# Attention row sums: fewer tile pairs summed by DMA, partition folds set further apart, the last folds done on 32 rows in DRAM

## The chip, the cores and the metric

The kernel runs on one core of one Trainium2 chip. The metric is the device time of one execution in microseconds; three runs of the kernel before give a median of 1814.33 us (1810.88 to 1819.57). TensorE (PE in the profile) multiplies, ScalarE (ACT) computes exponentials and copies out of PSUM, VectorE (DVE) adds, GpSimd (POOL) and SyncE (SP) issue DMAs. Each engine works through its own queue in the order of the program and waits on semaphores of the others.

## The reference

A gated mixture: attention over 32 heads of width 32 and a layer of small experts, mixed by a gate per token. What the change touches is the softmax's denominator in `_A_ref`, the sum of `exp(scores)` over the 2048 keys, for each head and query:

```python
x = A_x                                                  # 1 x 2048 x 1024
g = _sigmoid((x * gate_w).sum(-1, keepdims=True))
# _A_ref
qkv = (x @ wqkv).reshape(B, S, 3, H, Dh).transpose(2, 0, 3, 1, 4)    # H = 32, Dh = 32
scores = jnp.einsum("bhqd,bhkd->bhqk", q, k) * (Dh ** -0.5)
p = _softmax(scores, axis=-1)
a = jnp.einsum("bhqk,bhkd->bhqd", p, v).transpose(0, 2, 1, 3).reshape(B, S, D) @ wo
# _B_ref: two top-1 choices of 8 for each of 32 router heads, one of 64 experts, gelu(x . u_e) * v_e
return g * a + (1 - g) * b
```

## The kernel before

The kernel computes the projections first (to about 630 us of the span), then attention head by head (to about 1624 us), then the output product with `wo`. All of the program's order is written out by hand; the tile framework adds the semaphores.

**Attention.** For a head `h` the keys are in 16 tiles of 128 (`NT` = 16), the queries in 4 quarters of 512 (`NQ` = 4). One tile of one head is one *step*; step `k = h * 16 + kt`, 512 steps in all. `scores` (L1289 and L1298) multiplies a key tile by the queries, a quarter at a time, into a ring of seven PSUM banks, and ScalarE writes the exponentials as a tile `P[h, kt]` of 128 keys x 2048 queries (1 MB). `pv` (L1310) multiplies the tile by the values. Scores and `pv` are issued alternately in batches of about nine quarters; after each batch the actions due at the steps that it finished are issued (`at(step, f, ...)` puts them there, the list `todo` holds them), and then `presum` for the step itself. So the step of an action sets its place in every queue, and each queue keeps that order.

**Row sums.** The sum of `P[h, :]` over all keys is made in three levels.

1. *Over the 16 tiles.* VectorE adds tile after tile into `ACC[h]` (`presum` and `add`, L1351: two instructions of 128 x 1024 for each tile). Some pairs of tiles are first added by DMA: `accumulate(h, b, a)` (L1340) has GpSimd's queue add `P[h, a]` to `P[h, b]` in place, four steps after `b`'s number as listed (at `base + b + 4`), and VectorE adds the sum later (`add_pair`, and `merge` for the last pair). `pairs_of` names the pairs: (0, 2), (4, 6), (8, 10) in a head with three, (0, 2), (8, 10) in a head with two. Before, the odd heads below 28 have two, the others three; head 31 has its own. The tiles that are in no pair are added at their own step. `merge_odd` of head 29 is two adds of 64 partitions, each as long as one of 128.
2. *Over the 128 partitions of `ACC[h]`.* `fold(h, n)` (L1368) is a DMA on GpSimd's queue that adds partitions n to 2n - 1 to partitions 0 to n - 1; each fold waits for the one before it. Before: n = 64, 32, 16, then `store_rows` (L1372) writes 16 partitions to DRAM, `SED[g]`. Four heads make a group `g`.
3. *In DRAM.* `fold_rows(g, n)` (L1375) adds rows n to 2n - 1 of the group to rows 0 to n - 1, a DMA from DRAM to DRAM: n = 8, 4, 2, 1. `load_r` reads the row that is left, and `norm_r` (L1406 and L1407) makes reciprocals, times the gate, and stores them (`RD`), to be multiplied into the attention output at the end.

Heads 28 to 31 go another way: `head_sums` and `rowsum` (L1323) sum over the partitions on TensorE, partly after `fold_odd` (L1363) put two heads in one tile.

**Places.** The tiles `P` live in 13 places, 11 from head 20 step 8 on, and 10 from head 27 step 11 on. `p_tile` gives a new tile the place whose planned end is nearest, `min(until)`; the planned end of a tile is its step plus 14 for the tile `b` of a pair, 10 for a tile `a`, 5 for any other. The plan is only a choice of place: the exponential that writes a tile waits until every reader of the place's earlier tile is done (VectorE's add, `pv`, the DMA that reads it).

**Queues.** GpSimd's queue issues the pair sums, folds, stores and row folds, in order; an issue that waits holds those behind it. SyncE's queue loads queries, keys and values of later heads, stores the heads' outputs and, before, issued `load_r`.

Of the kernel before, what the change touches and what calls it, by code (L numbers as in the profile page):

```python
# [17 lines left out]
S = 2048  # L18
# [14 lines left out]
def gated_mha_peer_kernel(ctx, tc, xT, wqkv, wv, wo, wq, k12, ug, v, out):  # L33
# [23 lines left out]
    SMD = [dram.tile([4, S], F32, name=f"smd{g}") for g in range(G)]  # L57
    SED = [dram.tile([16, 4, S], F32, name=f"sed{g}") for g in range(G - 1)]
    RD = dram.tile([G, 4, S], F32, name="rd")
# [1091 lines left out]
    def pairs_of(h):  # L1151
        if h == H - 1:
            return (2, 4), (2, 6)
        if h % 2 and h < H - 4:
            return (0, 2), (8, 10)
        return (0, 2), (4, 6), (8, 10)
# [213 lines left out]
    def store_rows(h):  # L1370
        g, j = divmod(h, 4)
        nc.gpsimd.dma_start(SED[g][:, j, :], ACC.pop(h)[:16])  # L1372

# [26 lines left out]
    def load_r(g):  # L1400
        R[g] = wk.tile([128, 128], F32, name="rr", bufs=1)[:, :64]
        dma(R[g], (SMD[g] if g == G - 1 else SED[g][0]).rearrange("j (b m) -> (j b) m", m=64))

    def norm_r(g):
        r = R.pop(g)
        nc.vector.reciprocal(r, r)  # L1406
        nc.vector.tensor_mul(r, r, G64)  # L1407
        dma(RD[g].rearrange("j (b m) -> (j b) m", m=64), r)
# [43 lines left out]
    def at(step, f, *a):  # L1452
        todo.setdefault(step, []).append((f, a))

    for h in range(H):
# [6 lines left out]
        if h < H - 1:  # L1462
            at(base + 12, add_pair, h, 0)
            if len(pairs_of(h)) == 3:
                at(base + NT + 1, add_pair, h, 1)
            at(base + NT, finish, h)
            at(base + NT + 5, merge_odd if h == H - 3 else merge, h)
            if h == H - 2:
                at(base + NT + 8, head_sums, h)
            elif h == H - 3:  # L1470
                at(base + NT + 7, fold_odd, h)
                at(base + NT + 14, head_sums, h - 1, 2)
# [344 lines left out]
```

## Time and profile before

| | us |
|---|---|
| median of three runs | 1814.33 |
| lowest, highest run | 1810.88, 1819.57 |
| profiled execution | 1813.28 |
| its span | 1811.1 |
| TensorE, ScalarE, VectorE, GpSimd busy in it | 1798.6, 1218.4, 1485.4, 299.6 |
| DMA bytes moved | 361.66 MB |

The span runs from the first to the last instruction of the profiled execution; its time is 2.2 us longer. Busy time is counted over the whole span, although the stages differ: during attention TensorE, ScalarE and VectorE are all above 90%. A line of a timeline has start, length, engine, line, operation, what it writes and reads, how many instructions were merged into it, and in brackets the engine's idle time before it with what ended it. A line of a table of waits has who waited for whom, the sum in us, how often, and the longest. A line of DMA issues has destination and source, queue, how many, KB each, and the median from issue to landing.

### The profile page before, as it was taken

What the parts mean: (1) busy time and instruction counts of PE and PEld (TensorE: products, weight loads), DVE (VectorE), ACT (ScalarE), POOL (GpSimd) and SP (SyncE); (2) the same over time, 40 slices, a digit from 0 to 9 for tenths busy, and PEclk for the clock granted to TensorE, in tenths of its full rate; (3) what the DMA queues carried; (4) which work ended last, traced back from release to release, by engine and by line L of the source; (5) the groups of instructions that cost most, each with busy time, mean ns of one, the idle gap of its engine ahead of it and who ended that gap; (6) DMA issues with size and microseconds to landing.
All of it is one profiled execution on the core that took longest, in us unless ns stands there. A gap on an engine that the chain in (4) does not pass through costs nothing.

```text
span 1811.1 us, 27980 instructions
## 1 busy us (share of the span) xinstructions
PE 1798.6 (99%) x10567; PEld 1137.5 (63%) x10567; DVE 1485.4 (82%) x1656; ACT 1218.4 (67%) x1608; POOL 299.6 (17%) x370
## 2 busy tenths in 40 slices
PE   9999999999999999999999999999999999999999
PEld 7777777788888755555555555455544555447887
DVE  7868685368987689998989989898999898994584
ACT  4434422211233499999999999999999999992221
POOL 0222000026401211112112121121121211210000
PEclk9999999999999999999999999999999999999999
DMA  7788888723248689999999989999999899967871
GB/s 244 232 284 265 278 247 300 257 71 106 82 140 272 231 193 187 182 177 200 200 196 193 207 184 212 191 178 207 201 195 214 193 190 211 199 151 206 268 181 58
DMA packets 132753, 361.66 MB, mean 200 GB/s; under 512 B 18388, under 2 KB 58724, under 8 KB 107128
## 3 DMA queue, kind: packets, MB, share of 16 engines
q0 software_dynamic: 22752, 133.22, 38.7%
q1 hardware_dynamic: 89704, 190.71, 35.8%
q10 hardware_dynamic: 20160, 35.92, 6.8%
q8 instruction: 84, 1.38, 0.3%
q14 instruction: 53, 0.43, 0.1%
HBM read 172.58 MB, written 78.98 MB: 139 GB/s over the span
## 4 chain that ended last, share of the span: by engine, by line
PE 94%; DMA 3%; issue 1%; DVE 1%; ACT 1%; ACTq 0%; SPq 0%; DVEq 0%; POOL 0%; POOLq 0%
PE ring L1289 27%; PE o L1310 24%; PE bk L155 13%; PE bk L711 10%; PE pa L155 6%; PE bk L758 5%; PE bk L926 2%; PE pa L1561 2%; PE bk L311 2%; PE bk L491 1%; DMA P<-P 1%; PE bk L395 1%; DMA wo_raw<-P 1%; PE pa L1568 1%; DMA smd<-ssb 1%
## 5 line engine op out<-in xcount | busy, mean ns | idle before, releaser
L1298 ACT ACTIVATE P<-ring 128x512 f32<-128x512 f32 (+3 forms) x999 | 816.0, 938 | 17.8 <-PE ring L1289 9.6
L1351 DVE TENSOR_TENSOR acc<-acc,P 128x1024 f32<-128x1024 f32 x414 | 477.1, 1219 | 28.5 <-DMA P<-P 14.2
L1310 PE MATMUL o<-P,V 128*32 128x512 f32 (+1 forms) x4024 | 417.3, 534 | 0.0
L1289 PE MATMUL ring<-Q,K 98*128 98x512 f32 x1024 | 270.5, 407 | 1.7 <-ACT P L1298 1.7
L1289 PE MATMUL ring<-z,z 98*128 98x512 f32 x1020 | 267.4, 406 | 0.1
L1289 PEld LDWEIGHTS ring<-Q,K 98*128 98x128 f32 x1024 | 182.8, 188 | 120.9 <-ACT P L1298 42.1
L1289 PEld LDWEIGHTS ring<-z,z 98*128 98x128 f32 x1020 | 182.1, 188 | 114.7 <-ACT P L1298 40.0
L1310 PEld LDWEIGHTS o<-P,V 128*32 128x32 f32 x4024 | 111.7, 109 | 220.2 <-issue 200.4
L1351 DVE TENSOR_TENSOR rb<-rb,P 128x1024 f32<-128x1024 f32 x186 | 214.4, 1219 | 5.8 <-ACT P L1298 4.1
L240 ACT ACTIVATE hi<-bk 128x512 fp32r<-128x512 f32 x40 | 23.7, 594 | 120.4 <-PE bk L711 102.2
L1298 ACT ACTIVATE wo_raw<-ring 128x512 f32<-128x512 f32 (+3 forms) x110 | 100.4, 986 | 1.6 <-PE ring L1289 1.0
L711 PE MATMUL bk<-xh,e 128*128 128x512 f32 x384 | 94.2, 394 | 0.0
L1368 POOL DMA_DIRECT2D acc<-acc x58 | 48.3, 832 | 275.2 <-DMA acc<-acc 120.8
L711 PE MATMUL bk<-xl,e 128*128 128x512 f32 x384 | 92.2, 389 | 0.0
L711 PEld LDWEIGHTS bk<-xh,e 128*128 128x128 f32 x384 | 71.0, 188 | 22.0 <-issue 3.4
L253 DVE TENSOR_TENSOR lo<-bk,hi 128x512 fp32r<-128x512 f32 x40 | 27.6, 690 | 69.4 <-ACT hi L240 68.0
L1351 DVE TENSOR_TENSOR acc<-acc,wo_raw 128x1024 f32<-128x1024 f32 x56 | 65.9, 1219 | 21.4 <-DMA wo_raw<-P 16.8
L1340 POOL DMA_DIRECT2D P<-P x60 | 64.3, 1072 | 106.2 <-PE o L1310 51.0
L711 PEld LDWEIGHTS bk<-xl,e 128*128 128x128 f32 x384 | 72.1, 188 | 15.0
L101 DVE TENSOR_TENSOR e<-wraw,e 128x512 fp32r<-128x512 f32 (+3 forms) x64 | 54.9, 865 | 25.2 <-ACT e L100 24.7
L1298 ACT ACTIVATE vhl<-ring 128x512 f32<-128x512 f32 (+3 forms) x83 | 71.0, 939 | 0.2
L155 PE MATMUL bk<-xh,e 128*128 128x512 f32 x288 | 68.5, 393 | 0.0
(305 smaller groups left out, 2442.9 us busy)
## 6 DMA issues: line engine op xcount, KB each, us to landing
P<-P POOLq DMA_DIRECT2D x60, 1024.0 KB, 14.7
wqt<-in_wq SPq DMA_DIRECT2D x26, 1024.0 KB
wraw<-in_wqkv SPq DMA_DIRECT2D x30, 512.0 KB
acc<-acc POOLq DMA_DIRECT2D x20, 512.0 KB, 11.4
wo_raw<-P POOLq DMA_DIRECT2D x10, 1024.0 KB, 14.9
qdh<-hi ACTq DMA_DIRECT2D x32, 256.0 KB
qdl<-lo ACTq DMA_DIRECT2D x32, 256.0 KB
kdh<-hi ACTq DMA_DIRECT2D x32, 256.0 KB
```

What stands on the lines that cost most here:

```text
L101: (on or nc.vector).tensor_tensor(out=lo, in0=src, in1=hi.bitcast(F32), op=OP.subtract)
L155: nc.tensor.matmul(ps, self.a[a][i][:, k, :], self.b[b][j][k], start=(not first and k == 0 and i == j == 0), stop=(k == HC - 1 and i == 1))
L311: nc.tensor.matmul(ps[32 * quad:32 * quad + 32, :], kpad[:, quad % 2, i, :], t[:, quad, :], start=(i == 0), stop=(i == 3))
L711: nc.tensor.matmul(ps, t[:, kc // HC, a, kc % HC], x_at(b, n, kc), start=first, stop=last)
L758: nc.tensor.matmul(ps, x_at(a, t // 4, kc)[:, tok], b, start=first, stop=last)
L926: nc.tensor.matmul(p, x_at(a, t // 4, kc)[:, tok], b, start=first, stop=last)
L1289: on_ring(nc.tensor.matmul(ring[:, i, :], K[:98, kt * 128:(kt + 1) * 128], Q[:98, qc * 512:(qc + 1) * 512], start=True, stop=True), i)
L1298: on_ring(nc.scalar.activation(P[h, kt][:, q0 * 512:(q0 + m) * 512].rearrange("p (a m) -> p a m", a=m), ring[:, i:i + m, :], AF.Exp, scale ...
L1310: nc.tensor.matmul(O[h][32 * qc:32 * qc + 32, c0:c1], Vt[g][:, kt, 32 * j:32 * j + 32], p[:, qc * 512 + c0:qc * 512 + c1], start=(kt == 0) ...
L1340: nc.gpsimd.dma_start(P[h, b], P[h, a], accum_op=OP.add)
L1351: nc.vector.tensor_add(out[:, c], a[:, c], b[:, c])
L1368: nc.gpsimd.dma_start(ACC[h][:n], ACC[h][n:2 * n], accum_op=OP.add)
```

## The change

- `pairs_of`: two pairs instead of three in heads 2, 6, 10, 14, 18, 22, 26 and 30. Only every fourth head and head 29 keep three; the tiles 4 and 6 of those eight heads are added by VectorE one by one.
- The sum of the first pair is taken at step 14 (three pairs) or 16 (two) instead of 12, the second at 18 instead of 17, the merge at 22 instead of 21, and the planned end of a tile `b` is 16 steps on instead of 14.
- Fold 64 stands at step 24 instead of 23, fold 32 at 32 instead of 28, the fold to 16 rows is gone, and the store, now of 32 rows, is at 40 instead of 37.
- In DRAM the folds are of 16, 8, 4 and 2 rows, eight steps apart instead of five (five in the last such group), and two rows are left. `load_r` reads both side by side, by GpSimd's queue in the last group, and `norm_r` adds them on VectorE.
- One load of reciprocals for the end (`load_rb`) stands at step 13 of head 31 instead of 8.

```diff
-    SED = [dram.tile([16, 4, S], F32, name=f"sed{g}") for g in range(G - 1)]
+    SED = [dram.tile([32, 4, S], F32, name=f"sed{g}") for g in range(G - 1)]
...
-        if h % 2 and h < H - 4:
+        if h % 4 and h != H - 3:
             return (0, 2), (8, 10)
         return (0, 2), (4, 6), (8, 10)
...
-        until[i] = k + (14 if kt in [b for b, _ in pairs] else 10 if kt in [a for _, a in pairs] else 5)
+        until[i] = k + (16 if kt in [b for b, _ in pairs] else 10 if kt in [a for _, a in pairs] else 5)
...
-        nc.gpsimd.dma_start(SED[g][:, j, :], ACC.pop(h)[:16])
+        nc.gpsimd.dma_start(SED[g][:, j, :], ACC.pop(h)[:32])
...
     def load_r(g):
-        R[g] = wk.tile([128, 128], F32, name="rr", bufs=1)[:, :64]
-        dma(R[g], (SMD[g] if g == G - 1 else SED[g][0]).rearrange("j (b m) -> (j b) m", m=64))
+        R[g] = wk.tile([128, 128], F32, name="rr", bufs=1)
+        if g == G - 1:
+            dma(R[g][:, :64], SMD[g].rearrange("j (b m) -> (j b) m", m=64))
+        else:
+            dma(R[g].rearrange("p (r m) -> p r m", r=2), SED[g][:2].rearrange("r j (b m) -> (j b) r m", m=64),
+                nc.gpsimd if g == G - 2 else nc.sync)
 
     def norm_r(g):
-        r = R.pop(g)
+        r = R[g][:, :64]
+        if g < G - 1:
+            nc.vector.tensor_add(r, r, R[g][:, 64:])
+        R.pop(g)
         nc.vector.reciprocal(r, r)
...
-            at(base + 12, add_pair, h, 0)
-            if len(pairs_of(h)) == 3:
-                at(base + NT + 1, add_pair, h, 1)
+            three = len(pairs_of(h)) == 3
+            at(base + (14 if three else 16), add_pair, h, 0)
+            if three:
+                at(base + NT + 2, add_pair, h, 1)
             at(base + NT, finish, h)
-            at(base + NT + 5, merge_odd if h == H - 3 else merge, h)
+            at(base + NT + 6, merge_odd if h == H - 3 else merge, h)
...
-                at(base + NT + 7, fold, h, 64)
+                at(base + NT + 8, fold, h, 64)
                 if g + 1 < G:
-                    at(base + NT + 12, fold, h, 32)
-                    at(base + NT + 17, fold, h, 16)
-                    at(base + NT + 21, store_rows, h)
+                    at(base + 2 * NT, fold, h, 32)
+                    at(base + 2 * NT + 8, store_rows, h)
         if j == 3 and g + 1 < G:
-            for i, n in enumerate((8, 4, 2, 1)):
-                at(base + NT + 26 + 5 * i, fold_rows, g, n)
-            at(base + NT + 46, load_r, g)
-            at(base + NT + 53, norm_r, g)
+            gap = 5 if g == G - 2 else 8
+            for i, n in enumerate((16, 8, 4, 2)):
+                at(base + 2 * NT + 14 + gap * i, fold_rows, g, n)
+            at(base + 2 * NT + 14 + 4 * gap, load_r, g)
+            at(base + 2 * NT + 14 + 5 * gap + (2 if gap == 5 else 0), norm_r, g)
...
-    at((H - 1) * NT + 8, load_rb, 0, KC - 2, KC - 1)
+    at((H - 1) * NT + 13, load_rb, 0, KC - 2, KC - 1)
```

More of the change, by code (lines that the diff above doesn't have):

```diff
@@ L1462, in gated_mha_peer_kernel @@
         if h < H - 1:
-            at(base + 12, add_pair, h, 0)
-            if len(pairs_of(h)) == 3:
-                at(base + NT + 1, add_pair, h, 1)
+            three = len(pairs_of(h)) == 3
+            at(base + (14 if three else 16), add_pair, h, 0)
+            if three:
+                at(base + NT + 2, add_pair, h, 1)
             at(base + NT, finish, h)
-            at(base + NT + 5, merge_odd if h == H - 3 else merge, h)
+            at(base + NT + 6, merge_odd if h == H - 3 else merge, h)
             if h == H - 2:
-                at(base + NT + 8, head_sums, h)
+                at(base + NT + 9, head_sums, h)
             elif h == H - 3:
-                at(base + NT + 7, fold_odd, h)
-                at(base + NT + 14, head_sums, h - 1, 2)
+                at(base + NT + 8, fold_odd, h)
+                at(base + NT + 15, head_sums, h - 1, 2)
             else:
-                at(base + NT + 7, fold, h, 64)
+                at(base + NT + 8, fold, h, 64)
                 if g + 1 < G:
-                    at(base + NT + 12, fold, h, 32)
-                    at(base + NT + 17, fold, h, 16)
-                    at(base + NT + 21, store_rows, h)
+                    at(base + 2 * NT, fold, h, 32)
+                    at(base + 2 * NT + 8, store_rows, h)
         if j == 3 and g + 1 < G:
-            for i, n in enumerate((8, 4, 2, 1)):
-                at(base + NT + 26 + 5 * i, fold_rows, g, n)
-            at(base + NT + 46, load_r, g)
-            at(base + NT + 53, norm_r, g)
+            gap = 5 if g == G - 2 else 8
[3 more added lines that the diff above has]
+            at(base + 2 * NT + 14 + 5 * gap + (2 if gap == 5 else 0), norm_r, g)
         if g + 1 < G:
```

## The prediction

> **What bounds the kernel now.** I read the page first, then the attention stage (about 633 to 1624 us) by windows of one head, then the chain of waits, then the timelines around each place where the chain leaves TensorE.
>
> ```profile
> PE 1798.6 (99%) x10567; PEld 1137.5 (63%) x10567; DVE 1485.4 (82%) x1656; ACT 1218.4 (67%) x1608; POOL 299.6 (17%) x370
> ```
> ```profile
> 1407.40:1438.30 30.90, 30.90 (x220) 15.67 (x216) 29.07 (x26) 30.46 (x42) 6.22 (x8) 1.00 0.86 185
> 1531.20:1562.20 31.00, 29.90 (x199) 13.90 (x195) 23.31 (x22) 27.27 (x33) 4.88 (x6) 0.94 1.02 193
> sum 990.60, PE 988.91 PEld 496.31 DVE 913.36 ACT 971.27 POOL 178.04; mean PE 30.90 PEld 15.51 DVE 28.54 ACT 30.35 POOL 5.56
> ```
>
> The columns after the times are PE, PEld, DVE, ACT and POOL busy, granted clock, DMA share, GB/s. Over 32 heads TensorE is idle 1.7 us of 990.6. Nothing in the change takes a matmul away, so attention can be shortened only where TensorE was held up. The chain has one block of ten score matmuls per head, which serves as a clock:
>
> ```profile
> 850.20 2.59 PE ring L1289 x10
> 881.14 2.60 PE ring L1289 x10
> ...
> 1221.76 2.60 PE ring L1289 x10
> ...
> 1315.15 2.59 PE ring L1289 x10
> ...
> 1439.06 2.59 PE ring L1289 x10
> 1470.83 2.60 PE ring L1289 x10
> 1501.78 2.59 PE ring L1289 x10
> 1521.78 19.73 DMA P<-P
> ...
> 1567.40 2.60 PE ring L1289 x10
> ```
>
> Twelve heads from 850.20 to 1221.76 take 30.96 us each, 1.935 us a step (16 steps to a head). 1221.76 to 1315.15 is 0.5 over three such heads, 1439.06 to 1470.83 0.8 over one, 1501.78 to 1567.40 3.7 over two. **Held up: 5.0 us in all**, and 3.7 of it is one event:
>
> ```profile
> 1519.80 0.78 POOL L1368 DMA_DIRECT2D acc<-acc  x1 [10.89 <-PE o L1310]
> 1521.78 0.90 POOL L1340 DMA_DIRECT2D P<-P  x1 [1.20 <-ACT P L1298]
> 1529.58 0.78 POOL L1368 DMA_DIRECT2D acc<-acc  x1 [6.90 <-DVE acc L1351]
> ```
> ```profile
> 1541.59 1.88 ACT L1298 ACTIVATE P<-ring 128x2048 f32<-128x2048 f32 x1 [1.43 <-DMA P<-P]
> ```
> ```profile
> 1541.70 0.73 PE L1289 MATMUL ring<-Q,K 98*128 98x512 f32 x2
> 1543.52 2.95 PE L1289 MATMUL ring<-Q,K 98*128 98x512 f32 x7 [1.10 <-ACT P L1298]
> 1546.41 3.17 PE L1310 MATMUL o<-P,V 128*32 128x512 f32 x16
> ```
> ```profile
> 1532.16 2.36 DVE L1351 TENSOR_TENSOR rb<-P,P 128x1024 f32<-128x1024 f32 x2 [0.61 <-ACT P L1298]
> 1541.60 2.36 DVE L1351 TENSOR_TENSOR acc<-acc,P 128x1024 f32<-128x1024 f32 x2 [7.08 <-DMA P<-P]
> ```
>
> The mark at 1501.78 stands at step 4.5 of head 28, so its tile 10 is written 6.5 steps on, at 1514.4. The pair DMA of tiles 8 and 10 goes out at 1521.78, right behind the 32-row fold of head 27 (which waits for fold 64 to land; its row names a matmul that ended just then), and lands at 1541.5. ScalarE needs the place of one of its tiles and waits 1.43; TensorE then idles 1.10 and runs its next matmuls slowly (the window's clock is 0.94). So 1.43 us of waiting cost 3.7: 2.3 on top. The 0.5 is a place that VectorE gave back late, without a slow clock, at 1285 us: 0.4 us of ScalarE's waiting cost 0.5.
>
> ```profile
> ACT P L1298 <- DVE rb L1351: 0.4, 1, 0.4
> ```
>
> **The change part by part.** *POOL queue.* The 16-row fold is gone for 28 heads, and fold 64, fold 32 and the store now stand eight steps (15.5 us) apart. Before, each stood five steps (9.7 us) behind a DMA that it waits for, with the pair DMAs queued behind it:
>
> ```profile
> POOL acc L1368 <- DMA acc<-acc: 120.8, 19, 10.6
> POOL sed L1372 <- DMA acc<-acc: 83.5, 14, 10.5
> POOL rb L1368 <- DMA rb<-rb: 65.6, 11, 9.6
> ```
> ```profile
> P<-P POOLq DMA_DIRECT2D x60, 1024.0 KB, 14.7
> acc<-acc POOLq DMA_DIRECT2D x20, 512.0 KB, 11.4
> acc<-acc POOLq DMA_DIRECT2D x19, 256.0 KB, 7.8
> acc<-acc POOLq DMA_DIRECT2D x19, 128.0 KB, 9.9
> sed<-acc POOLq DMA_DIRECT2D x19, 128.0 KB, 9.0
> sed<-sed POOLq DMA_DIRECT2D x7, 256.0 KB, 8.9
> sed<-sed POOLq DMA_DIRECT2D x7, 128.0 KB, 13.0
> ```
>
> With 15.5 us between them a fold of 11.4 and one of 7.8 are down before the next asks, so pair DMAs go out when due: in head 28 at about 1514.4, not 7 us later. Pair sums get 10 to 12 steps (19.4 to 23 us) from issue to use instead of 8 or 9 (15.5 to 17.4), against 14.7 to land. The wait of 7.08 and the 3.7 go, and most likely the 0.5 and the 0.8 with them: **-5.0 us**. Bounds: -5.0, since no more was lost, and 0, if the same waits come back elsewhere. Eight pair DMAs of 1 MB and 28 folds of 128 KB go; 28 stores double to 256 KB, and the row folds of a group grow from 480 to 960 KB: 8.0 + 3.5 - 3.5 - 3.3, so the queue's bytes fall by nearly 5 MB, which the bound of 5.0 already holds.
>
> *VectorE.* Each head that loses a pair adds one tile more, eight heads in all. The pace, twenty halves without a break:
>
> ```profile
> 1543.88 22.79 DVE L1351 TENSOR_TENSOR rb<-rb,P 128x1024 f32<-128x1024 f32 x20
> ```
>
> That is 2.28 us a tile. A head with three pairs needs 12 adds (27.4 us), with two 13 (29.6) of 30.96, so VectorE still fits; the eight added sums cost 0 while the matmuls cover them (18.2 us if they did not). The extra 128x64 sum in norm_r is nearest to the multiply beside it, seven times 0.22 us, off the path:
>
> ```profile
> 1602.23 0.22 DVE L1407 TENSOR_TENSOR rr<-rr,G 128x64 f32<-128x64 f32 x1
> ```
>
> *Places.* This is where I see the cost. A tile's place is taken by a later tile, and ScalarE may write there only when the last reader is done. I laid out the rule of p_tile with the new 16/10/5. In a two-pair head the first pair sum is now VectorE's last item at step 16. VectorE works from the end of the exp of step 3 (1.9 us after it begins, as in the 128x2048 row above) through 13 adds: done 1.9 + 29.6 = 31.5 us after step 3 began, and its place goes to step 3 of the next head, 30.96 after, in heads 27 and 28 (ten or eleven places; earlier heads have at least a step more). About 0.7 us of waiting with the hand-over, twice. At the price of the small holds (0.4 cost 0.5) **+1.6 us**; bounds 0 (the ring's seven banks absorb it) and +6 (each draws the 2.3 of slow clock).
>
> Head 30 is worse. Between step 3 of head 30 and its own first pair sum VectorE has 14 adds: eleven single steps, two for merge_odd of head 29, and the sum itself: done at 1.9 + 31.9 = 33.8. The place goes to step 2 of head 31, 15 steps on: 29.0, plus the row sums put in before it:
>
> ```profile
> 1589.06 1.04 PE L1323 MATMUL ring<-acc,ones 128*32 128x512 f32 x8
> ```
>
> 30.1, so ScalarE waits about 3.8 us. Before, that head had 9 adds for singles, and the last of its pairs was due a step later into step 4. With the slow clock of the 1541 event, 3.8 + 2.3 = **+6.1 us**; bounds +2 (the ring hides most, no slow clock) and +9.
>
> *Fold behind the merge.* The merge moves from step 5, ahead of that step's add, to step 6, behind it: fold 64 and the next pair DMA wait in POOL's order until about 11 us after step 3 in a three-pair head; before, the pair went out about 8 after. Landing 14 to 18 later (14.7 median; eight pairs fewer speak for the short end), tile 6 of head 29 is free at 25 to 29; step 0 of head 30 wants it 13 steps on, at 25.2. Bounds 0 and +4 + 2.3; I take **+1.0**.
>
> *DRAM rows.* Sixteen rows of 32 KB are folded, then 8, 4 and 2. The first is bounded by 8.9 (256 KB) and twice that; with steps of 8 (15.5 us) nothing queues behind it, and with 5 in the last group it can hold POOL by up to 8 us, which the pair of head 30 can take. 0 here, a rival below.
>
> *End.* VectorE's last sum and the row sums that need it:
>
> ```profile
> 1617.80 9.16 DVE L1351 TENSOR_TENSOR acc<-acc,P 128x1024 f32<-128x1024 f32 x8
> ```
> ```profile
> 1627.47 1.92 PE L1323 MATMUL o<-P,ones 128*32 128x512 f32 x16
> 1629.21 1.04 PE L1323 MATMUL o<-acc,ones 128*32 128x512 f32 x8
> ...
> 1652.79 2.07 PE L1561 MATMUL pa<-woh,z 128*128 128x512 f32 x4 [4.16 <-ACT z L100]
> ```
>
> The sum is done at 1627.0, TensorE asks at 1629.2: 2.2 us spare, about one add, and the wait in head 31 gives VectorE time to catch up. Bounds 0 and +1; 0.
>
> Sum: -5.0 + 1.6 + 6.1 + 1.0 = **+3.7 us**. The profiled execution took 1813.28 (span 1811.1 and 2.2 around it), which gives 1817.0; the median of the runs, 1814.33, lies 1.05 above it, so I forecast **1818.0**.
>
> The Trainium skill ("TensorE: Matmul & The Clock Gate", Part 1) has the matmul clock fall to half only after an idle window of about 3.4 us, and rise again after as long. The trace disagrees: 1.10 us of idle was followed by slow matmuls. By that rule the wait of 3.8 alone would be slow, for one window at half rate, an estimate of 1.7 us in place of 2.3, and the sum +3.1.
>
> **The rivals.** (1) *The new waits do not bind*: TensorE runs seven banks ahead and ScalarE's wait is swallowed, while the old 5.0 goes. For it: 1.7 us idle in 990. Against it: 1.43 of ScalarE's waiting cost 3.7. -5.0 + 1.5 gives 1811. (2) *Places run out late*, the one on the slower side: from head 25 with ten or eleven places the pair DMAs of tiles 4 and 6, sent 3 us later, land 18 after; steps 1 of head 29 and 0 of head 30 wait 2 and 4 us, each with 2.3 of slow clock, 10.6 in place of 1.0: +13.3, 1828. It decides once such a pair lands more than 14 us after issue; the median of 14.7 speaks for it, the emptier queue against. (3) *The row folds are late*: the last group's chain of four, 13.0 each, plus its load exceed the 27 steps (52 us) up to norm_r, which stands before VectorE's adds of head 31; 4 x 13.0 and 7.8 for the load (as the 256 KB fold) are 60, 8 us late, 1826. Against it: the 256 KB row fold landed in 8.9, and 4 x 8.9 + 7.8 fits. (4) *Nothing happens*: the old waits return in the same size, 1814.
>
> **How the numbers follow.** Forecast 0.48, (1) 0.20, (2) 0.22, (3) 0.05, (4) 0.05. About 0.5% (9 us) is what this measurement can tell from no change. The forecast's own range is 1813 to 1823; reaching to (1) and most of (2) gives 1809 to 1829. Faster needs 1805.3, more than all that was held up: 0.04, for gains I do not see. Slower, above 1823.4: most of (2) and (3), the upper end of the forecast: 0.29. The rest is 0.67.
>
> **What would show it.** Right: the marks 30.96 apart up to head 26; POOL's waits for acc<-acc and rb<-rb near nothing; no wait of VectorE for P<-P; waits of ScalarE's P on VectorE's acc or rb of some 0.7 us near 1467 and 1498 and of about 4 near 1595, the last with a clock below 1. Wrong: no such wait near 1595, or a wait on DMA P<-P near 1557, or marks that spread before head 20.

## The result, and the profile after

| | before | after |
|---|---|---|
| median of 22 runs each, side by side | 1814.53 us | 1816.63 us |
| lowest, highest run | 1810.21, 1822.80 | 1812.08, 1819.19 |
| ratio after to before, 95% interval | | 1.0007 (0.9997 to 1.0017) |
| profiled execution, its span | 1813.28, 1811.1 us | 1816.48, 1814.7 us |
| VectorE, GpSimd busy in it | 1485.4, 299.6 us | 1503.8, 270.8 us |

No difference that this measurement can tell; the forecast was 1818.0. (The ratio is estimated from all runs; it is not the quotient of the two medians, 1.0012, which lies inside its interval.) The small result is made of two larger terms, and the profile shows both. First the marks of the chain of waits, one block of ten score matmuls per head, in the changed kernel:

```profile
1222.74 2.59 PE ring L1289 x10
...
1315.65 2.59 PE ring L1289 x10
...
1439.62 2.59 PE ring L1289 x10
1470.58 3.07 PE ring L1289 x10
1502.04 3.22 PE ring L1289 x10
1533.65 2.60 PE ring L1289 x10
1564.65 2.59 PE ring L1289 x10
```

1222.74 to 1315.65 is 30.97 a head, and so it goes on to 1470.58: the 0.5 at head 21 and the 0.8 at head 26 are gone. So is the 3.7 behind head 28 (1533.65 to 1564.65 is 31.0). New are 0.5 and 0.65 (31.46 and 31.61 for one head, with longer blocks at their start). GpSimd's waits and its DMAs' landings (tables of waits and of DMA issues, attention stage) say why the old ones went:

```profile
POOL acc L1368 <- DMA acc<-acc: 8.5, 7, 2.1
POOL rb L1368 <- DMA rb<-rb: 2.6, 2, 2.2
```
```profile
P<-P POOLq DMA_DIRECT2D x59, 1024.0 KB, 9.6
acc<-acc POOLq DMA_DIRECT2D x20, 512.0 KB, 5.4
```

120.8 us of waiting for acc<-acc are 8.5 now, 65.6 for rb<-rb are 2.6, and the same 1 MB pair DMA lands in 9.6 us instead of 14.7. VectorE has no wait for a DMA left in attention. ScalarE waits for a place three times, and each time for VectorE; its timeline:

```profile
1468.84 1.88 ACT L1298 ACTIVATE P<-ring 128x2048 f32<-128x2048 f32 x1 [0.60 <-DVE rb L1351]
...
1500.45 1.88 ACT L1298 ACTIVATE P<-ring 128x2048 f32<-128x2048 f32 x1 [0.76 <-DVE acc L1351]
...
1596.23 0.60 ACT L1298 ACTIVATE P<-ring 128x512 f32<-128x512 f32 x1 [4.50 <-DVE acc L1351]
```

Step 3 of heads 27 and 28, step 2 of head 31, as laid out. (TensorE's row sums of heads 28 to 30, `head_sums` with `fold_odd`, also stand one step later, which the list of the change leaves out.) VectorE's timeline shows that it never rests ahead of the third: nine adds on end, the pair sum of head 30 as the last of them.

```profile
1575.61 20.53 DVE L1351 TENSOR_TENSOR acc<-acc,P 128x1024 f32<-128x1024 f32 x18
1596.05 2.36 DVE L1351 TENSOR_TENSOR acc<-P,P 128x1024 f32<-128x1024 f32 x2
```

TensorE's timeline there; of ScalarE's 4.50 us of waiting 3.39 and 0.23 reach it:

```profile
1596.88 0.74 PE L1289 MATMUL ring<-Q,K 98*128 98x512 f32 x1 [3.39 <-ACT P L1298]
1597.85 0.79 PE L1289 MATMUL ring<-Q,K 98*128 98x512 f32 x1 [0.23 <-ACT P L1298]
1598.58 3.64 PE L1310 MATMUL o<-P,V 128*32 128x512 f32 x16
1602.15 2.86 PE L1289 MATMUL ring<-Q,K 98*128 98x512 f32 x8
1604.94 1.92 PE L1310 MATMUL o<-P,V 128*32 128x512 f32 x16
```

The same sixteen matmuls take 3.64 us and, six microseconds on, 1.92. **Attention as a whole**, from the first exponential of its stage to the copy of the last head's output, is a length that every experiment below is read by. In the changed kernel:

```profile
628.07 2.15 ACT L1298 ACTIVATE P<-ring 128x512 f32<-128x512 f32 x2 [1.62 <-PE ring L1289]
...
1629.08 0.60 ACT L1387 ACTIVATE osb<-o 128x512 f32<-128x512 f32 x1 [1.66 <-PE o L1310]
```

1001.0 us; before, 1624.66 - 627.29 = 997.4 by the same two rows. That is +3.6, where the sum of the prediction was +3.7; how its terms make it up is in the part on the prediction. From that copy to the end of the span, *the rest*, there are 185.6 us, before 186.5.

### The profile page after: what moved, and what is told of

It reads as the page before. It is cut to its first block, busy times and chain, and to the rows that moved or that the text cites. A ratio compares the mean times of both kernels' runs of the same rounds, so it can differ in the third digit from the quotient of the medians.

```text
span 1814.7 us, 27897 instructions
## 1 busy us (share of the span) xinstructions
PE 1799.9 (99%) x10567; PEld 1138.0 (63%) x10567; DVE 1503.8 (83%) x1679; ACT 1217.9 (67%) x1608; POOL 270.8 (15%) x335
## 4 chain that ended last, share of the span: by engine, by line
PE 96%; DMA 2%; ACT 1%; issue 1%; DVE 0%; SPq 0%; ACTq 0%; DVEq 0%
PE ring L1289 28%; PE o L1310 25%; PE bk L155 13%; PE bk L711 10%; PE pa L155 6%; PE bk L758 5%; PE bk L926 2%; PE bk L311 2%; PE pa L1569 2%; PE bk L491 1%; PE bk L395 1%; PE pa L1576 1%; ACT P L1298 1%; DMA wraw<-in_wqkv 1%; DMA smd<-ssb 1%
## 5 line engine op out<-in xcount | busy, mean ns | idle before, releaser
L1298 ACT ACTIVATE P<-ring 128x512 f32<-128x512 f32 (+3 forms) x990 | 807.9, 939 | 20.9 <-PE ring L1289 9.6
L1351 DVE TENSOR_TENSOR acc<-acc,P 128x1024 f32<-128x1024 f32 x420 | 484.1, 1220 | 22.1 <-ACT P L1298 22.0
L1351 DVE TENSOR_TENSOR rb<-rb,P 128x1024 f32<-128x1024 f32 (+1 forms) x188 | 217.2, 1220 | 8.4 <-ACT P L1298 8.4
L1340 POOL DMA_DIRECT2D P<-P x59 | 53.6, 909 | 469.5 <-PE o L1310 171.2
L1298 ACT ACTIVATE wo_raw<-ring 128x512 f32<-128x512 f32 (+3 forms) x119 | 105.7, 971 | 1.1 <-PE ring L1289 0.2
L1298 ACT ACTIVATE vhl<-ring 128x512 f32<-128x512 f32 (+3 forms) x83 | 72.8, 951 | 1.4 <-PE ring L1289 0.9
L100 ACT ACTIVATE e<-wraw 128x512 fp32r<-128x512 f32 (+3 forms) x64 | 44.7, 705 | 38.7 <-DMA wraw<-in_wqkv 22.5
```

What stands on the lines that cost most here:

```text
L100: nc.scalar.activation(hi, src, AF.Copy)
L1298: on_ring(nc.scalar.activation(P[h, kt][:, q0 * 512:(q0 + m) * 512].rearrange("p (a m) -> p a m", a=m), ring[:, i:i + m, :], AF.Exp, scale ...
L1340: nc.gpsimd.dma_start(P[h, b], P[h, a], accum_op=OP.add)
L1351: nc.vector.tensor_add(out[:, c], a[:, c], b[:, c])
```

## The experiments

Theory: the added time is ScalarE waiting for places whose last reader is a late pair sum, and the 5.0 us gained are GpSimd's queue, whose issues the change sets further apart (*the spread* below). Main rival: VectorE with 13 adds to a head is too full, whatever their order. Each run was timed beside the kernel before, which had medians of 1815.47 (sum14, sum14_h30, end20, spread_only), 1814.27 (pure_spread, pairs_only, late_h30, sum14_copy) and 1812.95 us (end21, spread_sum12, fold27, before_copy). Each group ran on another chip. So medians of different groups can differ by some 2.5 us for no reason in the kernel, and are better compared by how far each lies below the kernel before beside it. The table has what the profiles gave: attention and the rest as above, then the issue of one DMA near the end, the 1 MB copy `t3l<-t2l`, against the end of attention, and the time from the issue of the last row sums' store `smd<-ssb` (8 KB) to that of the load behind it, which waits for it to land. Both become important below. (Where the first expectations count "the stretch behind attention" at 178.5 us, they count to the last block of matmuls; the rest, to the end of the span, is about 7 us longer.)

| run | median us | ratio to before (95%) | attention | rest | copy issued | store to load |
|---|---|---|---|---|---|---|
| before | 1814.53 | | 997.4 | 186.5 | +4.8 | 10.4 |
| after | 1816.63 | 1.0007 (0.9997 to 1.0017) | 1001.0 | 185.6 | +4.9 | 10.5 |
| sum14 | 1808.95 | 0.9954 (0.9938 to 0.9970) | 992.6 | 185.4 | +4.9 | 10.5 |
| sum14_h30 | 1810.98 | 0.9973 (0.9957 to 0.9989) | 993.6 | 187.4 | +4.9 | 11.3 |
| late_h30 | 1819.04 | 1.0018 (1.0001 to 1.0036) | 1002.1 | 187.8 | +4.9 | 11.8 |
| end20 | 1809.35 | 0.9957 (0.9938 to 0.9977) | 992.7 | 186.0 | +4.0 | 12.4 |
| end21 | 1802.16 | 0.9941 (0.9920 to 0.9963) | 992.5 | 179.6 | -2.0 | 7.1 |
| pure_spread | 1810.19 | 0.9973 (0.9961 to 0.9985) | 993.5 | 186.6 | +4.8 | 10.7 |
| spread_only | 1805.33 | 0.9936 (0.9910 to 0.9961) | 995.6 | 179.9 | -3.5 | 7.1 |
| spread_sum12 | 1802.19 | 0.9941 (0.9919 to 0.9962) | 992.6 | 179.5 | -4.0 | 7.3 |
| pairs_only | 1809.20 | 0.9968 (0.9946 to 0.9989) | 998.1 | 182.8 | -0.1 | 8.8 |
| fold27 | 1814.02 | 1.0012 (0.9991 to 1.0033) | 992.9 | 188.4 | +4.9 | 12.3 |
| sum14_copy | 1806.36 | 0.9950 (0.9930 to 0.9970) | 992.8 | 184.9 | +26.6 | 9.2 |
| before_copy | 1813.20 | 1.0004 (0.9987 to 1.0021) | 1000.7 | 181.7 | +24.8 | 7.5 |

### The late pair sums

**sum14**, the changed kernel with

```diff
-            at(base + (14 if three else 16), add_pair, h, 0)
+            at(base + 14, add_pair, h, 0)
```

> The changed kernel with one number altered: in every head the first pair sum stands at step 14 in VectorE's order, as it already does in heads of three pairs, and not at step 16. Theory (the added time is the wait of ScalarE for places whose last reader is VectorE's last item): the pair sum is done two adds, 4.6 us, earlier; the waits of 0.6 and 0.76 us in heads 27 and 28 go, the wait of 4.5 in step 2 of head 31 falls below 0.7, the clock in that window comes back above 0.97, and the time is some 8 us below the changed kernel, near 1808.5, so 0.9965 of the kernel before, with the 5.0 us of the POOL queue's spread left as the gain. Rival (VectorE with 13 adds a head is simply too full, whatever their order): the same sums are only handed on, waits of the same size turn up at the places of later tiles, and the time stays within 2 us of 1816.6.

As the theory had it. VectorE does the same adds, in another order, and all three waits are gone: in ScalarE's table of waits the writing of `P` at L1298 has one line left, and it names TensorE.

```profile
ACT P L1298 <- PE ring L1289: 7.5, 31, 1.6
```

7.7 us of the median follow (1816.63 to 1808.95; 8.6 when each is set against the kernel before beside it), 8.4 of attention. VectorE's load is not what binds; the rival falls.

**sum14_h30**, the same in head 30 alone (`14 if three or h == H - 2 else 16`):

> The same edit in head 30 alone. Theory: the two small waits of heads 27 and 28 stay (0.6 and 0.76 us, some 1.2 us of time) and only the 7.1 us at head 31 go, so about 7 us below the changed kernel, near 1809.6. Rival (the small waits weigh more than their length, as places that are late are handed on from head to head): 1811 to 1813. Rival (VectorE too full): 1816.6.

Attention is 993.6: 7.4 us less than in the changed kernel for head 31 alone. The waits of 0.6 and 0.8 us at heads 27 and 28 stay, and cost 993.6 - 992.6 = 1.0. The time, 1810.98, is 1.4 above the 1809.6 expected; it would fit the first rival's 1811 as well. Attention decides: it is where the theory has it, and the profiled execution is longer in the rest, whose store took 11.3 us here.

**late_h30**, head 30's first pair sum one tile later still:

```diff
-            at(base + (14 if three else 16), add_pair, h, 0)
+            at(base + (14 if three else 18 if h == H - 2 else 16), add_pair, h, 0)
```

> The changed kernel with the first pair sum of head 30 one tile add later still in VectorE's order (behind the first sum of head 31). Theory (ScalarE's wait in step 2 of head 31 is this sum's lateness, and time follows it one for one): the wait grows from 4.5 to 6.8 us, and the time by 2.3 us, to 1818.9; the slow clock behind it stays at about 2.5 us. Rival (the wait is set by something else, VectorE's load in all or a DMA): wait and time as in the changed kernel. Rival (a longer idle stretch of TensorE costs more in slow clock): over 4 us more.

The wait is the sum's lateness, to the tenth: 6.75 us, one add of 2.28 more than 4.50.

```profile
1598.51 0.60 ACT L1298 ACTIVATE P<-ring 128x512 f32<-128x512 f32 x1 [6.75 <-DVE acc L1351]
```

The time came out as expected (1819.04, +2.4), but not for the reason given. Between the two profiled executions, which are 3.3 apart, attention grew by 1.1 us only; the other 2.2 are in the rest, with a store of 11.8 us, and what part of those is chance stays open. Why attention grew by half of the wait is in TensorE's timeline and in its granted clock, microsecond by microsecond. This run:

```profile
1599.16 0.80 PE L1289 MATMUL ring<-Q,K 98*128 98x512 f32 x1 [5.67 <-ACT P L1298]
1600.14 0.79 PE L1289 MATMUL ring<-Q,K 98*128 98x512 f32 x1 [0.18 <-ACT P L1298]
1600.87 3.26 PE L1310 MATMUL o<-P,V 128*32 128x512 f32 x16
```
```profile
1596.00:1597.00 1.00, 0.00 (x0) 0.00 (x0) 1.00 (x2) 0.00 (x0) 0.00 (x0) 0.90 0.02 8
1597.00:1598.00 1.00, 0.00 (x0) 0.00 (x0) 1.00 (x2) 0.00 (x0) 0.00 (x0) 0.50 0.00 0
...
1603.00:1604.00 1.00, 1.00 (x8) 0.00 (x0) 1.00 (x2) 0.33 (x1) 0.00 (x0) 0.69 0.41 129
```

and the changed kernel:

```profile
1596.00:1597.00 1.00, 0.12 (x1) 0.13 (x1) 1.00 (x2) 0.77 (x2) 0.00 (x0) 0.98 0.00 0
1597.00:1598.00 1.00, 0.77 (x2) 0.26 (x2) 1.00 (x2) 1.00 (x3) 0.00 (x0) 0.50 0.00 0
...
1603.00:1604.00 1.00, 1.00 (x4) 0.77 (x4) 0.00 (x0) 0.74 (x2) 0.00 (x0) 0.61 0.99 329
```

The clock (third figure from the end) falls to one half near 1597 and returns near 1603.7 in both, although TensorE began again at 1596.88 in the one and at 1599.16 in the other. A share of 0.98 and 0.61 in the outer slices makes 0.04 + 6 + 0.78 = 6.8 us at half clock in the changed kernel, 0.20 + 6 + 0.62 = 6.8 here. What a wait costs on top is half of the part of that stretch in which TensorE works. Changed kernel: 3.6 us idle and about 3.3 lost to the clock, 6.9; here 5.85 idle and about half of 1599.2 to 1603.6 lost, less the 0.18, so 2.1: 8.0. The difference is the 1.1 measured. That the half clock stood at the same moments in both executions is not explained by this; the table under "The clock" below shows that in other places it begins sooner or later.

**end20** and **end21**, the changed kernel with one number altered, VectorE's order left as it is:

```diff
-        until[i] = k + (16 if kt in [b for b, _ in pairs] else 10 if kt in [a for _, a in pairs] else 5)
+        until[i] = k + (20 if kt in [b for b, _ in pairs] else 10 if kt in [a for _, a in pairs] else 5)
```

> The changed kernel with VectorE's order as it is, and the planned end of a pair-sum's place at 20 steps in place of 16, so that places are handed out in another order. Theory (only which tile takes which place is wrong, not VectorE's load or order): laid out by the rule, the place of each first pair sum goes to a tile at least 2 us behind its sum, no wait of ScalarE for VectorE above 0.3 us is left, and the time is near 1808, 0.996 of before. Rival (the order of VectorE is what is late, and with 10 places some tile must wait): waits of 1 us or more at other steps of heads 28 to 31, 1812 or above.

Attention is 992.7 and no wait for VectorE is left. So a late sum is harmless where its place goes to a later tile: what cost time was the sum and the plan together, a planned end of 16 steps for sums that VectorE has done 19 to 21 steps on (31.5 us after step 3 in heads 27 and 28 as the prediction has it, 34 in head 30, at 1.935 us a step). The time missed its 1808 by 1.3; the rest takes 186.0 here. The end of this run is in the next part, with end21.

### GpSimd's queue

**pure_spread**, the changed kernel with the pairs, planned ends and pair-sum steps of before:

```diff
-        if h % 4 and h != H - 3:
+        if h % 2 and h < H - 4:
...
-        until[i] = k + (16 if kt in
+        until[i] = k + (14 if kt in
...
-            at(base + (14 if three else 16), add_pair, h, 0)
+            at(base + 12, add_pair, h, 0)
...
-                at(base + NT + 2, add_pair, h, 1)
+                at(base + NT + 1, add_pair, h, 1)
```

> The changed kernel with the pairs, the planned ends of places and the times of the pair sums of the kernel before; what is left of the change is POOL's spread queue, the merge and fold 64 one step later, and the 32 stored rows. Theory (the 5.0 us held up in attention come from POOL's queue, and the 8.6 us of new waits from the later pair sums with the added tiles): the wait of 1.43 us at 1541 on DMA P<-P is gone, POOL's waits for acc<-acc fall from 120.8 us to below 20, no wait of 4.5 in head 31; the layout of places gives waits of 0.8 and 1.4 us in head 30 at most, so attention is 992.4 to 996 us long against 997.4 before and 1001.0 in the changed kernel. The stretch behind attention stays as before (178.5 to 180 us), since the 1 MB copy t3l<-t2l waits for tile 14 of the last head as before: 1809.5 to 1813. Rival (the spread gains nothing without the eight pairs fewer): attention 997 us or more, 1814 or more.

Its lines in the tables of waits:

```profile
POOL acc L1368 <- DMA acc<-acc: 12.4, 9, 2.3
```
```profile
ACT P L1298 <- DVE acc L1351: 1.0, 1, 1.0
```

Attention 993.5, the 1810.19 within what was expected: the spread, with the merge one step later and the 32 stored rows that go with it, takes 3.9 us out of attention, 4.9 if the one wait of 1.0 that the layout leaves is counted at its length.

**pairs_only**, the kernel before with the new `pairs_of` and nothing else (the first two lines of the diff above, the other way round).

> The kernel before with only the choice of pairs changed (eight heads with two pairs in place of three; POOL's order, the 16 rows and the pair sums as before). Theory (POOL's bunched queue is what holds attention up): POOL still waits over 90 us for acc<-acc, and the pair DMA of tiles 8 and 10 of head 28 still goes out behind the fold of head 27 near 1521; attention 993 to 998 us. Behind attention: by the layout, the place under the 1 MB copy t3l<-t2l holds tile 10 of the last head in place of 14, so the copy starts by 1622 and not at 1629, the last row sums' store smd<-ssb goes by it in about 7 us in place of 10.4, and the stretch behind attention is about 5 us shorter: 1804 to 1810 in all. Rival (the end does not depend on the copy, and the short end of the run of the spread alone came from VectorE being done sooner): the end stays at 178.5 us or more, 1810 to 1815.

```profile
POOL acc L1368 <- DMA acc<-acc: 136.6, 25, 13.0
```
```profile
ACT P L1298 <- DMA P<-P: 3.6, 2, 1.8
```

Eight pair DMAs fewer leave GpSimd's waits as they were, and ScalarE still waits for pair DMAs; attention, 998.1, is no shorter. The gain in attention is the spread's. What this profiled execution gains comes from the end: 182.8 us, 3.7 less where 5 were expected (the copy went out at the end of attention, not some 3 us ahead of it).

**fold27**, the kernel before with three issues of head 27 alone sent three steps later, behind the pair DMA that they held up:

```diff
-                    at(base + NT + 12, fold, h, 32)
-                    at(base + NT + 17, fold, h, 16)
-                    at(base + NT + 21, store_rows, h)
+                    at(base + NT + (15 if h == 27 else 12), fold, h, 32)
+                    at(base + NT + (20 if h == 27 else 17), fold, h, 16)
+                    at(base + NT + (24 if h == 27 else 21), store_rows, h)
```

> The kernel before with the folds of 32 and 16 rows and the store of head 27 alone sent three steps later, behind the pair DMA of tiles 8 and 10 of head 28 in place of ahead of it. Theory (the pair DMA that waits behind that fold is what holds up attention near 1541): the pair DMA goes out near 1515 in place of 1521.8, the wait of 1.43 us on DMA P<-P is gone with the slow clock behind it, the mark of head 30 comes 61.9 to 62.2 us after that of head 28 in place of 65.6 (31 for each head), attention is 3.7 us shorter, 993.7, and the time about 1811. Rival (the pair DMA is slow because of all the traffic, not because of the fold ahead of it): it lands at 1541 or later all the same and the wait stays.

The profile shows all that was expected: the pair DMA is out at 1515.33, ScalarE waits for no DMA, the marks of heads 28 and 30 are 61.97 apart, attention is 992.9.

```profile
1515.33 0.86 POOL L1340 DMA_DIRECT2D P<-P  x1 [7.31 <-ACT P L1298]
```
```profile
1501.62 2.59 PE ring L1289 x10
...
1563.59 2.59 PE ring L1289 x10
```

The time does not: median 1814.02, runs from 1810.58 to 1824.00, no gain that can be told. A profiled execution shows the waits of that one execution, one draw. That the draws differ is seen in before_copy (below), whose attention is the kernel before's, instruction for instruction: there one wait for a pair DMA is 3.96 us long, at another place, and attention takes 1000.7 instead of 997.4.

```profile
1532.15 2.37 ACT L1298 ACTIVATE P<-ring 128x2048 f32<-128x2048 f32 x2 [3.96 <-DMA P<-P]
```

The scatter of the times agrees with this, though it does not show that the waits are what scatters. In the four kernels with the crowded queue (before, pairs_only, fold27, before_copy) the lowest and the highest of 12 to 29 runs lie 11 to 19 us apart; in those with the spread queue, of 6 to 12 runs, 0.6 to 2.8, and in the 22 runs of the changed kernel 7.1.

### The end

**spread_only**, the changed kernel with the pairs of before (the first two lines of the diff of pure_spread).

> The changed kernel with the pairs of the kernel before (sixteen heads... heads of three pairs as before, all of heads 28 to 30 among them), so that POOL's spread queue and the 32 stored rows are alone. Theory: the spread alone takes POOL's waits for acc<-acc from 120.8 us to below 20 and those for rb<-rb from 65.6 to below 10, and the wait of 1.43 us on DMA P<-P at 1541 goes (-5.0 us in all); head 30 then has 12 adds and the wait of 4.5 in head 31 is gone too. Against that stand three waits that the layout of places gives, 1.2 us at step 3 of head 28 and 1.8 at step 0 of heads 29 and 30, 5 us without slow clock and up to 10 with it: 1811 to 1819, with the waits to be seen there. Rival (the 5.0 us come from fewer pair DMAs, not from the spread): the waits on DMA P<-P are back at heads 28 and 29, POOL's waits above 60 us.

The attention came as expected, with GpSimd's waits gone and waits of 0.64 us at head 28 and 1.23 at head 30 in ScalarE's timeline; at head 29 the 1.30 us that ScalarE waits are put down to TensorE. It takes 995.6 us, 3 more than sum14. Yet the run is 3.6 us *faster* than sum14, at the low end of what was expected: its rest is 5.5 us shorter. Nothing in the prediction or in this expectation speaks of that. SyncE's timeline shows where it comes from. The changed kernel:

```profile
1633.97 0.34 SPq L82 DMA_DIRECT2D t3l<-t2l  x1
...
1637.43 0.51 SPq L82 DMA_DIRECT2D smd<-ssb  x1
1647.91 0.32 SPq L82 DMA_DIRECT2D rr<-smd  x1
```

spread_only:

```profile
1620.03 0.34 SPq L82 DMA_DIRECT2D t3l<-t2l  x1
...
1629.85 0.50 SPq L82 DMA_DIRECT2D smd<-ssb  x1
1636.93 0.32 SPq L82 DMA_DIRECT2D rr<-smd  x1
```

The last row sums go to DRAM and back through this queue, and TensorE has other work for only so long: in the kernel before it then stood still for 4.16 us (shown in the prediction, at 1652.79). The 8 KB store takes 10.5 us from issue to the load behind it where a 1 MB copy of output weights (prepared from blocks of `wo`) went out 3.5 us ahead of it, and 7.1 where the copy went out ten. The copy's destination takes the memory of old places, so it waits for their last readers. In spread_only the last it waited for was a pair DMA (the table of SyncE's waits says so); in end20 it was the row-sum matmuls of the last head:

```profile
SPq L82 <- DMA P<-P: 2.4, 1, 2.4
```
```profile
SPq L82 <- PE o L1323: 5.9, 1, 5.9
```

So which of the last tiles lies under the copy decides, and that comes out of `min(until)`.

**sum14_copy**, sum14 with the copy sent later:

```diff
-    load_t(2, 1, [fin.tile([128, S], F32R, name="t3l")])
+    t3l = fin.tile([128, S], F32R, name="t3l")
...
         load_t(0, n, raw_place(n))
+    load_t(2, 1, [t3l])
```

> The changed kernel with the first pair sums at step 14, and the 1 MB copy t3l<-t2l sent behind the last loads of the normalisation and not ahead of the last head's row sums. Theory (behind attention the path is row sums to DRAM, back, reciprocal, to DRAM and back; the copy that runs at the same time makes the store of 8 KB take 10.4 us in place of 7): the store lands in about 7 us, TensorE's wait of 4.0 us for z falls below 1, its slow matmuls behind it go, and the stretch behind attention shrinks from 178.5 to about 173, so 1803.5 in all. Rival (the copy only moves the collision, to the loads that follow or to its own use near 1676): 1808 or more, with a new wait of TensorE for t3l or V.

Half right. TensorE's wait for z falls from 4.0 to 1.5, but the time gains little: the median is 2.6 lower than sum14's, 1.4 when each is set against the kernel before beside it, and the rest is 0.5 shorter. The store still takes 9.2 with no copy ahead of it. GpSimd's loads beside it are no sufficient reason, since before_copy and end21 have them too with stores of 7.5 and 7.1; what slowed it stays open. And the rival is right about the other half: the copy now goes ahead of the next block's loads. VectorE waits for them until 1670.67, 50 us after the end of attention, and TensorE further on. The rows are VectorE's and TensorE's timelines of this run, then VectorE's of end21, where the same instruction comes 41.7 us after the end of attention.

```profile
1670.67 2.37 DVE L1622 TENSOR_TENSOR V<-V,P 128x1024 f32<-128x1024 f32 x2 [15.51 <-DMA P<-rd]
```
```profile
1692.96 0.50 PE L155 MATMUL pa<-woh,acc 128*128 128x512 f32 x1 [1.75 <-ACT acc L100]
```
```profile
1661.28 1.23 DVE L1622 TENSOR_TENSOR V<-V,P 128x1024 f32<-128x1024 f32 x1 [9.54 <-DMA P<-rd]
```

**before_copy**, the same edit in the kernel before:

> The kernel before with the 1 MB copy t3l<-t2l sent behind the last loads of the normalisation, as in the run that had this with the pair sums at step 14. Theory (the copy costs the kernel before at its end what it costs the changed one): attention as before, 997 us, the stretch behind it 184 to 185 in place of 186.5, with TensorE's wait for z at 1.5 us in place of 4.2; 1 to 3 us faster, 1812. Rival (the late start of the copy gained in that run by the other places only): same as before within 1 us.

The rest shrinks from 186.5 to 181.7 in the profile, more than expected, with a store of 7.5 and no wait of TensorE for z. The time shows nothing of it (1813.20 against 1812.95, no difference): most likely the draws of attention, with runs from 1807.39 to 1819.12, cover it, and this profiled execution had a bad one.

**end21**, end20 with 21 in place of 20:

> The changed kernel with the planned end of a pair sum's place at 21 steps in place of 16, and nothing else. By the layout no tile waits for its place (all have 3 us or more), as with 20 steps, so attention takes 992.6 us as there; but the tiles of the last head come to lie in other places, with tiles 6 and 11 under the 1 MB copy t3l<-t2l, in place of 2 and 14 (16 steps) and 11 and 15 (20 steps). Theory (the stretch behind attention is set by when that copy goes out, and that by the last reader of the tiles under it): the copy starts ahead of the last head's end as in the run of the spread alone, the store smd<-ssb takes 7 to 9 us in place of 10.5, TensorE waits under 2 us for z, the stretch behind attention takes 180 to 183 us in place of 185.6, and the time is 1803 to 1806. Rival (the copy's start does not matter; the end of the run of the spread alone came from something else in it): 1808 to 1810, as with 20 steps.

Right, and better than expected: 1802.16. Its SyncE timeline:

```profile
1617.62 0.34 SPq L82 DMA_DIRECT2D t3l<-t2l  x1
...
1626.46 0.50 SPq L82 DMA_DIRECT2D smd<-ssb  x1
1633.56 0.32 SPq L82 DMA_DIRECT2D rr<-smd  x1
```

end20 and end21 are the same program but for the places that tiles get. Attention is 992.7 and 992.5; the rest 186.0 and 179.6, with TensorE idle 4.53 us before its next product in the one and not at all in the other; the medians are 7.2 apart, 4.7 when each is set against the kernel before beside it. The runs in which the copy keeps its place in the queue fit by its start: at -4.0 to -2.0 the rest is 179.5 to 179.9, at -0.1 it is 182.8, at +4.0 to +4.9 it is 185.4 to 188.4. That the copy, and not another effect of the places, lengthens the store is what most of this points to; the 9.2 of sum14_copy does not fit, and that copy alone was not slowed or shrunk in a run of its own.

**spread_sum12**, spread_only with its first pair sums at step 12 in every head:

> The changed kernel with the pairs of the kernel before, and the first pair sum at step 12 in every head. It differs from the run of the spread alone only in that sum's step (14 or 16 there), so every tile has the same place. Theory (the waits in heads 28 to 30 of that run, 4 us of its time, are the lateness of this sum; its short end comes from where the last tiles lie): attention 992.5 us in place of 995.6, the stretch behind it 179.9 as there, 1802.3 in all, 0.993 of before. Rival (with three pairs in 19 heads the pair DMAs land too late for a sum at step 12): VectorE waits for P<-P, and the time is 1805 or more.

Right in all points: 992.6, 179.5, 1802.19 (the heads of three pairs are 17, not the 19 of the expectation). VectorE waits for no pair DMA, so none is too late for step 12. end21 and this run reach the same time by different ways; both are 10.8 us below the 1812.95 of the kernel before beside them, a ratio of 0.9941 with intervals well below 1.

## Why the prediction came out right, and where it did not

The mechanism was right: old holds go, and late pair sums make new ones at the places named. That the sum came within 0.1 of the +3.6 is in part luck. Head 31 was 1.3 too small, heads 27 and 28 were 0.5 and the fold behind the merge 1.0 too large, and these misses nearly cancel.

- **What is removed, -5.0.** Right for the execution it was read from: with no holds left attention takes 992.5 us (end21), so before had 4.9 too much, by GpSimd's queue (pure_spread) and not by the number of pairs (pairs_only). But the prediction took one execution's holds for the kernel's. They change from run to run (997.4 and 1000.7 for the same attention), and a single fold moved away, the one named at 1541, gained nothing that can be told. The step from the profiled execution to the median, +1.05, did not carry over: in the changed kernel the median is 0.15 above the profiled execution (1816.63 and 1816.48), and the missing 0.9 is most of the 1.4 by which the forecast was high.
- **Heads 27 and 28, +1.6.** The waits are there, 0.60 and 0.76 us for the 0.7 forecast; they cost 1.15 by the marks, 1.0 by sum14_h30. Mis-sized by 0.5: no slow clock followed, and TensorE had no idle time at all.
- **Head 31, +6.1.** The right sum, tile, step and engine. ScalarE waited 4.50 for 3.8, and it cost 7.4. The 3.8 came from whole adds counted from the exponential of step 3 and a place asked for at 30.1; VectorE was done at 1596.1, which counted back from the mark at 1564.65 (step 4.5) is 34.4 us after step 3 where the prediction had 33.8. The 2.3 on top of ScalarE's wait, taken from the 1541 event, was 2.9. By the working under late_h30, 3.6 us of idle TensorE and 3.3 of slow clock give 6.9 of the 7.4; the last 0.5 is not accounted for.
- **The fold behind the merge, +1.0.** Nothing: no wait near 1557. The pair DMAs land in 9.6 us (median) and not 14 to 18. The prediction had used 14.7, a landing time from the crowded queue, for the emptied one, although it named the emptier queue as speaking for the short end.
- **VectorE, DRAM rows, end, 0 each.** VectorE took 18.4 us more work, and it is its order that told and not its load (sum14); the row folds of 512 and 256 KB landed in 11.4 and held up neither VectorE nor TensorE (GpSimd waited 13.8 us for two of the last group's); the rest is 0.9 shorter. The end's 0 was right as a difference, and blind as a reading: 6 to 7 us lay there in both kernels (185.6 and 186.5 against 179.6). The prediction quoted the 4.16 us of TensorE's idling at 1652.79, used the row only to show VectorE's slack, and did not ask what the wait was for.
- **Rivals.** (1), waits that do not bind: they bind, 7.4 us for one. (2), places late through pair DMAs: no such wait, a median landing of 9.6. (3), late row folds: VectorE waited for none. (4), the old waits back: gone.
- **The clock.** The 6.8 and the 3.4 us at half clock (6.8 above; before, near 1541, the microseconds from 1545 to 1549 have 0.78, 0.50, 0.50 and 0.52, so 0.44 + 2 + 0.96) are two and one times 3.4. That agrees with the length of the free-running window that the Trainium skill gives ("TensorE: Matmul & The Clock Gate", Part 1), 3413 ns. What that page of the Trainium skill says of the cause, a window that is idle, the trace does not bear out as it stands: in the kernel before 1.10 us of idle time within such a stretch was enough.

```profile
1545.00:1546.00 1.00, 1.00 (x3) 0.47 (x2) 1.00 (x2) 1.00 (x4) 0.99 (x2) 0.78 0.88 155
...
1548.00:1549.00 1.00, 1.00 (x12) 0.20 (x4) 1.00 (x2) 0.87 (x2) 0.00 (x0) 0.52 0.94 194
```

Nor does a longer idle time make a longer stretch, as other places of these traces show, worked out in the same way from their slices of one microsecond:

| run | TensorE idle, us | until | half clock begins, us after the idle time began | at half clock, us |
|---|---|---|---|---|
| spread_only | 0.68 | 1526.06 | | 0 |
| pairs_only | 1.01 | 1419.24 | | 0 |
| before | 1.10 | 1543.52 | 3.1 | 3.4 |
| pairs_only | 1.46 | 1545.54 | 1.9 | 3.4 |
| before_copy | 3.20 | 1534.08 | 2.3 | 6.8 |
| after | 3.39 | 1596.88 | 3.5 | 6.8 |
| sum14 | 4.03 | 1648.62 | 3.9 | 3.4 |
| before | 4.16 | 1652.79 | 2.7 | 6.8 |
| end20 | 4.53 | 1649.72 | 5.3 | 3.4 |
| late_h30 | 5.67 | 1599.16 | 3.3 | 6.8 |

The stretch comes in two lengths, and the length of the idle time does not tell which. So 2.3 us on top of a wait was not a price that could be carried from one wait to the next. What decides between the two lengths, and between a stretch and none, is not shown; it may be when the idle time falls, and not how long it is.

## What to carry to other kernels

A buffer plan that says when a place will be free must be moved together with the work that frees it: here one number, 16 to 21, took 8.5 us out of attention with the order of the work untouched. The 6 us that it took out of the end are another matter: they come from which tiles then lie under the copy, and nothing in a choice between 20 and 21 aims at that. A stall that is read from one profiled execution is one draw where a crowded queue makes it; the run-to-run scatter says whether it is a fixed price. And a stage that a change leaves alone still deserves its question, what does the bound engine wait for there, since a better gain may lie in it than in the change.

## What was not expected of the hardware

The landing time of a DMA depends on how its queue is scheduled. The same 1 MB pair sum has a median of 14.7 us with issues bunched and of 11.0 with them spread and the pairs the same (pure_spread); with eight pairs fewer it is 13.9 bunched (pairs_only) and 9.6 spread.

```profile
P<-P POOLq DMA_DIRECT2D x60, 1024.0 KB, 11.0
```

An 8 KB store took 7.1 to 7.3 us from issue to the load that waits for it where a 1 MB copy had gone out 8.8 to 10.3 us ahead of it, 8.8 at 7.0 us ahead, and 10.4 to 12.4 at 2.9 to 3.5 us; with no copy ahead it took 7.5 and 9.2. And in late_h30 a longer idle time of TensorE was dearer by less than its length (2.25 us more of ScalarE's waiting, 1.1 us more of attention), since part of the half-rate stretch passed while TensorE still stood still; this is one pair of profiled executions.
